# Tile 0's scores as two products of 64 stationary columns, moved in front of tile 0's V product

## The chip, the cores and the metric

The kernel runs on one core of one Trainium2 chip. The metric is the device time of one execution in microseconds (us), the median of several runs.

Five engines work side by side: TensorE (PE: matrix products and transposes; PEld is its loading of stationary operands), VectorE (DVE), ScalarE (ACT), GpSimd (POOL) and SyncE (SP, which issues most of the DMAs). Each takes its instructions in the program's order.

## What is computed

Block-causal attention with 8 batches, 8 heads, 576 positions and a head size of 64, followed by a mixture of 8 experts, of which each position takes one:

```python
scores = scale * np.matmul(q, k.transpose(0, 1, 3, 2))
mask = block_i >= block_j
scores = np.where(mask, scores, -1000000000.0)
attn = np.exp(scores - np.max(scores, axis=-1, keepdims=True))
attn = attn / (np.sum(attn, axis=-1, keepdims=True) + 1e-09)
attn_out = np.matmul(attn, v)
...
expert_idx = np.argmax(x @ w_gate, axis=1)
for e in range(E):
    xe = x[expert_idx == e]
    out[expert_idx == e] = gate_w * (np.maximum(xe @ w1[e], 0.0) @ w2[e])
```

A block has 64 positions, so the 576 positions are 9 blocks. All of it is in float32 or in float32 split into two parts.

## The kernel before, in words

**Attention** works on 32 pairs of heads (m = 0 to 31, 4 pairs for each batch). The 9 blocks of a head are cut into tile 0 (the first 64 positions) and tiles 1 to 4 (128 positions each). The operations of a pair are named steps, and the table `ORDER` (line 414) writes them out by hand. `run` (line 360) goes through the table once per turn, 36 turns in all; an entry such as `S0:3` does step S0 for the pair m = turn - 3. So a turn works on several pairs at once, and pair m has its step with the number 3 in turn m + 3. No scheduler moves anything: the order of the table is the order of each engine's instructions. Entries that begin with z or y let in single steps of the experts' routing and of weight preparation.

The steps that matter here:

- `ld` (line 97, SyncE): loads qd (the queries, with the first block of the keys behind them), kd and v of a pair. qd has three buffers, so the load for pair m waits until the last reader of pair m - 3 is done. That reader is S0 of pair m - 3, in the same turn.
- `pQ` (line 109, GpSimd): scales 640 columns of qd into q. q has two buffers, so this waits for S0, the last reader of the q from two pairs earlier, in the same turn too.
- `S0` (line 157, TensorE): tile 0's scores. The 128 stationary columns of q are head a's 64 positions and head b's 64; in each, the rows of the other head are zero, so one product over all 128 rows gives both heads' scores, one above the other (128 x 64). A float32 product is two TensorE instructions (two passes).
- `S1` to `S4` (line 160): scores of tiles 1 to 4, head a on the rows 0 to 63 and head b on 64 to 127.
- `T..` (line 215): transposes of the exponentials, 128 stationary columns; `H..` (line 244) copies them from PSUM on ScalarE or VectorE. Ta1 is the group directly behind V5 and O0; Tt0 is tile 0's transpose.
- `V0` to `V4` and `V5` (line 253): products with the values. Each is one product for head a and one for head b, each with 64 stationary columns; head a writes the PSUM partitions 0 to 63, head b 64 to 127. V5 is tile 0's: both of its products have 64 moving columns.
- `O0` (line 279, VectorE) copies V5's result out; `M0` (VectorE) takes the maximum of S0's scores, `E0` (ScalarE) their exponential; `Z` (GpSimd) scales tile 0's exponentials into p.

The results of V5, S0, F1 and, in a second allocation, F2 and F0 lie in one PSUM bank (tag o2, one buffer, `part`, line 121). Whichever of S0 and V5 comes first in a turn opens the bank anew and waits for the readers and writers of the turn before.

A turn begins with the last exponential of the pair before (E3B) and ends with the V products V0 to V4. In front of V5 on TensorE thus stand the products of V4, and S1 to S3 ahead of V0.

When a batch is done, `sink` (line 1514) puts its next work in the queues: after the first batch (in turn 7) ten zero fills (line 1517: nine of 256.5 KB and a single row) and three loads of weights (line 1502) on SyncE's queue, behind the load of that turn.

**The experts** (from line 1570 on) come after the attention, with their own loops; the change doesn't touch them.

Of the kernel before, what the change touches and what calls it, by code (L numbers as in the profile page):

```python
# [17 lines left out]
P = 128  # L18
H = 8
S = 576  # L20
D = 64
# [17 lines left out]
class Attention:  # L39
# [113 lines left out]
    def op_S(self, m, i):  # L153

        mm = self.nc.tensor.matmul
        q, k = self.qs[m], self.raws[m][1]
        if i == 0:
            mm(self.part(1, m, "S0", 432, 496), q[:, 512:], self.raws[m][0][:, 512 + P :], start=True, stop=True)  # L158
            return
        e = 64 + 128 * i  # L160
        for c in range(2 if i == 4 else 1):
            for j in range(2):
                out, _ = self.region(m, i, j)
                if i == 4:
                    out = out[:, c]
                n = out.shape[-1]
                o = (0 if j else S - e) + n * c
                r = slice(64 * j, 64 * j + 64)
                ins = mm(  # L169
                    out, q[r, 128 * (i - 1) : 128 * i], k[r, o : o + n], start=True, stop=True, skip_group_check=True  # L170
                )
                self.uses(m, i, j, ins)
# [239 lines left out]


ORDER = """
E3B:3 V5:4 z2:0 O0@D:4 ld:0 Ta1:3 O@A:4 Ha1@A:3 S0:3 S4:2 z6:0 M0:3 Tb1:3 Tk0:3 pQ:1 K4B:2 E0:3 R1:3 K4A:2 z1:0 M4B:2
R2:3 F1:4 Hb1@A:3 Ta2:3 Hk0@A:3 X1:4 Y1:4 M4A:2 Tb2:3 F2:4 E4B:2 y0:0 Z:3 Hb2@D:3 F0:4 Ha2@A:3 Y2:4 z4:0 Tx3:3 Tt0:3
E4A:2 X2:4 S1:2 z5:0 z0:0 z3:0 Ht0@A:3 Y0@D:4 S2:2 K1A:2 K2A:2 S3:2 K1B:2 Hx3@A:3 K2B:2 V0:3 V2:3 M2A:2 K3A:2 M1B:2
M3A:2 E2A:2 E1B:2 V1:3 y1:0 E3A:2 V3:3 M1A:2 K3B:2 M2B:2 E1A:2 M3B:2 V4:3 E2B:2
# [1174 lines left out]
```

## Time and profile before

| | us |
|---|---|
| median of 3 runs | 817.57 |
| the three runs | 817.12, 817.57, 820.97 |
| the profiled execution | 815.47 |
| its span in the profile | 813.7 |
| TensorE busy | 785.0 (96%) |
| VectorE busy | 474.0 (58%) |
| ScalarE busy | 399.5 (49%) |
| GpSimd busy | 391.5 (48%) |

The profile is of one execution; its times count from the start of its span, and 1.8 us of the execution lie outside of it. Busy shares are means over the attention half (to about 372 us) and the expert half. TensorE's records overlap, since products are pipelined: the distance from one start to the next is what a product costs in a row of products, and its duration is longer than that. A number in square brackets behind a row is idle time of the engine before it, and what ended it.

### The profile page before, as it was taken

The numbers are of one execution on the slowest core, as the hardware profiler recorded it, in microseconds if no ns is written. First come the engines' busy times: TensorE is split into PE (matmuls) and PEld (weight loads), VectorE is DVE, ScalarE is ACT, GpSimd is POOL, SyncE is SP. The second block draws the span as 40 slices with busy tenths as digits, with TensorE's granted clock in tenths as the row PEclk, the third lists the DMA queues.
The fourth block names the chain that finished last, engine by engine and source line by source line (L and its number), as shares of the span: only waits on it lengthen the run. The fifth ranks groups of instructions, "written<-read, shape, count | busy, mean of one in ns | idle before, by whom it ended". The sixth has DMA issues, their size and how long they took to land.

```text
span 813.7 us, 17547 instructions
## 1 busy us (share of the span) xinstructions
PE 785.0 (96%) x4524; PEld 590.0 (73%) x4524; DVE 474.0 (58%) x1316; ACT 399.5 (49%) x1016; POOL 391.5 (48%) x397
## 2 busy tenths in 40 slices
PE   4999999999999999998999999999999999999995
PEld 2667666667776666666878888888888888888873
DVE  3666666776767677756846764412244713566953
ACT  3777777777787777762432333232332222332231
POOL 4122243344444361435456766555555556656753
PEclk9999999999999999999999999999999999999999
DMA  4239843536363626541447676744455654667772
GB/s 164 97 101 168 203 125 125 120 121 166 118 156 104 153 76 153 161 120 31 151 120 213 204 209 172 230 131 122 119 154 181 171 182 119 194 210 234 224 214 63
DMA packets 71120, 123.65 MB, mean 152 GB/s; under 512 B 16449, under 2 KB 37697, under 8 KB 70978
## 3 DMA queue, kind: packets, MB, share of 16 engines
q1 hardware_dynamic: 49858, 87.84, 38.2%
q0 software_dynamic: 7680, 20.50, 8.1%
q10 hardware_dynamic: 13440, 13.78, 6.3%
q8 instruction: 45, 0.74, 0.4%
q14 instruction: 97, 0.79, 0.3%
HBM read 73.09 MB, written 21.98 MB: 117 GB/s over the span
## 4 chain that ended last, share of the span: by engine, by line
PE 69%; issue 10%; POOL 9%; DMA 5%; ACT 2%; ACTq 1%; SPq 1%; DVE 1%; POOLq 1%; DVEq 0%
PE py L1170 14%; PE o L270 11%; PE pt L1009 7%; PE ya L169 7%; PE o L1009 4%; PE ph L1009 4%; PE xa L169 4%; PE o L305 4%; POOL low L1143 3%; POOL out L1192 2%; DMA xd<-xg 2%; ACTq L1120 1%; DMA qd<-qT 1%; ACT pb L200 1%; PE o L299 1%
## 5 line engine op out<-in xcount | busy, mean ns | idle before, releaser
L1170 PE MATMUL py<-w,low 128*128 (+1 forms) x912 | 219.7, 396 | 3.2 <-POOL low L1143 1.9
L1170 PEld LDWEIGHTS py<-w,low 128*128 128x128 f32 x912 | 170.5, 187 | 45.6 <-POOL low L1143 2.3
L112 POOL TENSOR_SCALAR q<-qd 128x640 f32<-128x640 f32 x32 | 57.9, 1810 | 188.4 <-PE o L158 124.3
L1188 ACT ACTIVATE y<-py,gates 128x512 f32<-128x512 f32 x35 | 24.1, 689 | 190.7 <-issue 106.3
L1143 POOL TENSOR_TENSOR low<-high,low 128x512 fp32r<-128x512 f32 x69 | 98.0, 1442 | 12.5 <-ACT low L1135 12.1
L1009 PE MATMUL pt<-w,high 128*128 x408 | 98.0, 395 | 0.0
L1009 PEld LDWEIGHTS pt<-w,high 128*128 128x128 f32 x408 | 76.4, 187 | 18.6
L1331 DVE TENSOR_TENSOR w<-raw,w 128x1024 f32 x48 | 74.1, 1582 | 0.0
L200 ACT ACTIVATE pb<-ya,neg 128x320 f32<-128x320 f32 (+2 forms) x96 | 50.0, 524 | 48.1 <-DVE neg L185 48.1
L1087 DVE STREAM_TRANSPOSE hblk<-xg 128x512 f32<-128x512 f32 x35 | 24.8, 710 | 82.5 <-DMA xg<-xd,idx 79.1
L169 PE MATMUL ya<-kd,q 64*128 64x192 f32 (+2 forms) x192 | 61.8, 457 | 2.7 <-ACT pb L200 2.7
L169 PE MATMUL yb<-kd,q 64*128 64x192 f32 (+2 forms) x192 | 61.8, 456 | 0.0
L1328 DVE CAST w<-raw 128x1024 f32 x48 | 52.8, 1140 | 15.1 <-issue 13.2
L695 POOL DMA_INDIRECT tab<-toks,posi x40 | 41.5, 1036 | 28.5 <-DVE run L662 14.8
L1099 DVE STREAM_TRANSPOSE hblk<-pt 128x512 f32<-128x512 f32 x34 | 23.7, 709 | 49.9 <-ACT pt L1046 49.7
L916 POOL DMA_INDIRECT xg<-xd,idx x39 | 43.2, 1108 | 19.3 <-POOL idx L908 18.0
L978 POOL TENSOR_TENSOR xl<-high,xh 128x512 fp32r<-128x512 f32 x16 | 21.2, 1328 | 62.0 <-ACT xh L968 62.0
L200 ACT ACTIVATE pb<-yb,neg 128x192 f32<-128x192 f32 (+2 forms) x96 | 49.7, 525 | 0.2 <-DVE neg L185 0.2
L978 POOL TENSOR_TENSOR high<-high 128x512 fp32r<-128x512 f32 x17 | 24.3, 1431 | 50.5 <-ACT high L968 50.5
L169 PE MATMUL xa<-kd,q 64*128 64x288 f32 x128 | 41.6, 447 | 6.5 <-POOL q L112 6.5
L1135 ACT CAST low<-high 128x1024 fp32r<-128x1024 f32 x35 | 36.5, 1043 | 19.0 <-DMA high<-hblk 17.6
L1192 POOL DMA_INDIRECT out<-y,idx x35 | 38.8, 1108 | 12.9 <-ACT y L1188 5.5
(1015 smaller groups left out, 1760.9 us busy)
## 6 DMA issues: line engine op xcount, KB each, us to landing
raw<-w SPq DMA_DIRECT2D x52, 512.0 KB, 4.7
high<-hblk SPq DMA_DIRECT2D x280, 48.0 KB
high<-hblk ACTq DMA_DIRECT2D x280, 48.0 KB
qd<-qT SPq DMA_DIRECT2D x32, 352.0 KB, 3.6
v<-vt SPq DMA_DIRECT2D x32, 352.0 KB, 4.6
kd<-kT SPq DMA_DIRECT2D x32, 288.0 KB, 3.7
xd<-xt SPq DMA_DIRECT2D x7, 1026.0 KB, 8.4
xd<-xg SPq DMA_DIRECT2D x9, 256.5 KB, 12.8
```

Of the source, the lines that this page charges most:

```text
L112: self.nc.gpsimd.tensor_scalar(q, self.raws[m][0][:, 0 : 512 + P], 0.125, None, ALU.mult)
L169: ins = mm(out, q[r, 128 * (i - 1) : 128 * i], k[r, o : o + n], start=True, stop=True, skip_group_check=True)
L200: ins = self.nc.scalar.activation(dst, src, AF.Exp, bias=self.neg[m][:, c : c + 1], scale=1.0, accum_out=self.sums[m][:, c : c + 1])
L270: self.nc.tensor.matmul(out[r], self.raws[m][2][:, slot], self.ph[m, bank][:, c0:c1], start=t in (0, 5), stop=t in (4, 5), skip_group_chec ...
L916: pool.indirect_dma_start(out=self.xg[i], out_offset=None, in_=self.xd[:, :], in_offset=bass.IndirectOffsetOnAxis(ap=self.idx[:, t : t + 1 ...
L978: pool.tensor_sub(xl, r, xh).then_inc(sem["xp"], 1)
L1009: m = pe.matmul(ph[f], x[:, P * k : P * k + P], weights(k, f, part), start=start and k == 0, stop=stop and k == 3,)
L1143: engine.tensor_sub(hl[:, c], h[:, c], hh[:, c]).then_inc(sem["ln" if engine is pool else "le"], 1)
L1170: m = pe.matmul(self.py[t % 2], h[:, c // 4, P * (c % 4) : P * (c % 4) + P], wf[:, bass.ds(off + (base + 512 * c), 512)], start=n == 0, st ...
L1192: pool.indirect_dma_start(out=self.out[:, :], out_offset=bass.IndirectOffsetOnAxis(ap=(self.router.first if t < EARLY else self.idx)[:, t ...
L1328: dve.tensor_copy(part(c, 0), raw[c % 4]).then_inc(sem["wh"], 1)
L1331: dve.tensor_sub(part(c, 1), raw[c % 4], part(c, 0)).then_inc(sem["wd"], 1)
```

## The change

S0 is no longer one product of 128 stationary columns. It is two of 64, one for each head: head a's columns of q write the partitions 0 to 63, head b's 64 to 127, and both have the same 64 moving columns. It is still computed over all 128 rows with the same zeros. In the table S0 moves from its place between Ta1 and S4 to the place in front of V5.

```diff
         if i == 0:
-            mm(self.part(1, m, "S0", 432, 496), q[:, 512:], self.raws[m][0][:, 512 + P :], start=True, stop=True)
+            out = self.part(1, m, "S0", 432, 496)
+            for j in range(2):
+                r = slice(64 * j, 64 * j + 64)
+                mm(out[r], q[:, 512 + 64 * j : 576 + 64 * j], self.raws[m][0][:, 512 + P :], start=True, stop=True)
             return
...
 ORDER = """
-E3B:3 V5:4 z2:0 O0@D:4 ld:0 Ta1:3 O@A:4 Ha1@A:3 S0:3 S4:2 z6:0 M0:3 Tb1:3 Tk0:3 pQ:1 K4B:2 E0:3 R1:3 K4A:2 z1:0 M4B:2
+E3B:3 S0:3 V5:4 z2:0 O0@D:4 ld:0 Ta1:3 O@A:4 Ha1@A:3 S4:2 z6:0 M0:3 Tb1:3 Tk0:3 pQ:1 K4B:2 E0:3 R1:3 K4A:2 z1:0 M4B:2
```

The lines behind the first hunk stand 3 further down in the changed kernel (S4 is L172 there, V L273, the transposes L242).

TensorE's order from V4 of pair 16 to S4 of pair 18, with what each instruction waits for (a semaphore is named by the engine that raises it, DMAHW by a DMA queue). Before (V5 is the product out of h, S0 the one out of qd and q, Ta1 the row pt17a):

```order
L270 MATMUL o_2646<-ph16a_2618,v_2096 64x128
L270 MATMUL o_2646<-ph16b_2615,v_2096 64x128
L270 MATMUL o_2674<-h_130,v_2096 64x64 [waits DVE_49,PE_49]
L270 MATMUL o_2674<-h_130,v_2096 64x64
L239 MATMUL pt17a_2687<-ident,pb_2584 128x128 [waits Activation_49]
L239 MATMUL pt17a_2687<-ident,pb_2584 128x128 x3
L158 MATMUL o_2674<-qd_2247,q_2433 128x64 [waits DMAHW2_49,DVE_49]
L169 MATMUL xa_2697<-kd_2397,q_2575 128x288 [waits DMAHW2_49]
L169 MATMUL xb_2699<-kd_2397,q_2575 128x288 [waits Activation_49]
```

And in the changed kernel:

```order
L273 MATMUL o_2663<-ph16a_2635,v_2111 64x128
L273 MATMUL o_2663<-ph16b_2632,v_2111 64x128
L161 MATMUL o_2691<-qd_2263,q_2449 64x64 [waits DMAHW2_49,DVE_49,PE_49]
L161 MATMUL o_2691<-qd_2263,q_2449 64x64
L273 MATMUL o_2691<-h_130,v_2111 64x64 x2
L242 MATMUL pt17a_2706<-ident,pb_2601 128x128 [waits Activation_49]
L242 MATMUL pt17a_2706<-ident,pb_2601 128x128 x3
L172 MATMUL xa_2715<-kd_2414,q_2592 128x288 [waits DMAHW2_49,DVE_49]
L172 MATMUL xb_2717<-kd_2414,q_2592 128x288 [waits Activation_49]
```

S0's two products stand between V4 and V5 and have taken over V5's waits; S4 stands directly behind the transposes and has a wait for VectorE that S0 had covered.

VectorE's order at O0 (L281, L284 in the changed kernel) and M0 (the reduction out of o), in the same turn. Before:

```order
L281 COPY o_134<-o_2674 128x64 [waits PE_49]
L575 TENSOR_REDUCE L_2677<-lg_2156 128x32
L185 TENSOR_REDUCE neg_2582<-o_2674 128x1 [waits PE_49]
L180 MEMSET xb_2699 64x64 [waits PE_49,Activation_49]
L206 TENSOR_TENSOR rs_2583<-sums_2581,eps 128x9 [waits Activation_49]
```

And in the changed kernel:

```order
L284 COPY o_134<-o_2691 128x64 [waits PE_49]
L578 TENSOR_REDUCE L_2696<-lg_2170 128x32
L188 TENSOR_REDUCE neg_2599<-o_2691 128x1
L183 MEMSET xb_2717 64x64 [waits PE_49,Activation_49]
L209 TENSOR_TENSOR rs_2600<-sums_2598,eps 128x9 [waits Activation_49]
```

Nothing changes places there; M0 no longer waits for TensorE, since O0 ahead of it waits for a later product.

## Rows read from the trace of the kernel before

**Rows 1.** Stretches: window, busy time of each engine, granted clock, DMA share, GB/s

```profile
17.20:20.80 3.60, 3.53 (x14) 2.43 (x14) 0.59 (x2) 2.13 (x8) 1.81 (x1) 1.00 0.27 65
26.00:86.00 60.00, 60.00 (x449) 40.59 (x446) 39.43 (x153) 45.83 (x142) 11.36 (x11) 1.00 0.56 121
98.00:340.00 242.00, 241.90 (x1845) 168.19 (x1842) 169.18 (x692) 184.62 (x562) 101.69 (x97) 1.00 0.50 136
```

**Rows 2.** Timeline of TensorE in turn 20: start, duration, instruction, [idle before]

```profile
204.52 0.27 PE L270 MATMUL o<-ph16a,v 128*64 128x128 f32 x1
...
204.63 0.27 PE L270 MATMUL o<-ph16a,v 128*64 128x128 f32 x1
...
204.74 0.28 PE L270 MATMUL o<-h,v 128*64 128x64 f32 x4
204.79 0.23 PE L270 MATMUL o<-h,v 128*64 128x64 f32 x2
204.95 0.66 PE L239 MATMUL pt17a<-ident,pb 128*128 128x128 f32 x4
205.34 0.27 PE L239 MATMUL pt17a<-ident,pb 128*128 128x128 f32 x1
205.45 0.34 PE L158 MATMUL o<-qd,q 128*128 128x64 f32 x2
205.72 0.51 PE L169 MATMUL xa<-kd,q 64*128 64x288 f32 x1
```

**Rows 3.** Timeline of TensorE, later in this turn and at the next V5

```profile
207.38 0.60 PE L239 MATMUL pt17k<-ident,pb 128*128 128x128 f32 x4
207.82 0.66 PE L305 MATMUL o<-fold,oT 128*128 128x144 f32 x4
...
210.44 0.27 PE L236 MATMUL pt17t<-ident,p 128*64 128x128 f32 x1
210.65 0.43 PE L169 MATMUL ya<-kd,q 64*128 64x192 f32 x1
...
215.53 0.28 PE L270 MATMUL o<-h,v 128*64 128x64 f32 x4
```

**Rows 4.** Chain of work that ended last, turns 7 to 9: start, length, what

```profile
62.88 0.19 PE o L158 x2
...
63.12 0.33 SPq L104
...
68.28 13.27 DMA xd<-xg
...
81.62 7.22 DMA qd<-qT
```

**Rows 5.** Timeline of TensorE in turn 9, the transpose of pair 6

```profile
91.28 0.30 PE L236 MATMUL pt6t<-ident,p 128*64 128x128 f32 x1 [1.61 <-POOL p L213]
```

**Rows 6.** Timeline of TensorE, the router's small products in turn 21

```profile
219.15 0.24 PE L611 MATMUL o<-oh,ones 128*128 128x32 bf16 x4
219.25 0.31 PE L239 MATMUL pt18a<-ident,pb 128*128 128x128 f32 x1
```

**Rows 7.** Timelines of VectorE and GpSimd around S0 in turns 20 and 21

```profile
205.07 0.23 DVE L281 COPY o<-o 128x64 f32<-128x64 f32 x1 [0.33 <-PE o L270]
...
207.12 0.11 DVE L180 MEMSET xb<- 64x64 f32 x1 [1.07 <-PE xb L169]
...
216.61 0.23 DVE L185 TENSOR_REDUCE neg<-o 128x1 f32<-128x64 f32 x1 [0.53 <-PE o L158]
...
205.94 1.81 POOL L112 TENSOR_SCALAR q<-qd 128x640 f32<-128x640 f32 x1 [6.00 <-issue]
```

**Rows 8.** Timeline of TensorE in turn 3

```profile
17.27 1.11 PE L239 MATMUL pt0a<-ident,pb 128*128 128x128 f32 x4 [2.13 <-ACT pb L200]
...
18.64 0.85 PE L169 MATMUL xa<-kd,q 64*128 64x288 f32 x1
```

**Rows 9.** Chain of work that ended last, turns 33 and 34

```profile
355.14 2.70 ACT pb L200 x10
357.84 0.31 ACT oT L277
```

## The prediction

> **What bounds the kernel now.** The table of stretches comes first: from 26 to 86 us and from 98 to 340 us, the attention half, TensorE is busy all the time (60.00 of 60.00, 241.90 of 242.00) [rows 1]. There nothing counts but the length of TensorE's own row of products, and it counts in full, turn for turn. A turn is 10.79 us (tile 0's V product starts at 204.74 and in the next turn at 215.53 [rows 2, 3]).
>
> Next, the turn itself, product by product [rows 2]. Tile 4's V products (64 stationary columns) run as pairs of head a and head b: one pair at 204.52, the next at 204.63. Tile 0's V product (V5) is four instructions, two passes for each of two heads, with the same 64 stationary columns: one pair at 204.74, the other at 204.79, and at 204.95 the transposes, which use all 128 columns. Then the scores of tile 0 (S0, two passes, 128 stationary columns) from 205.45 to 205.79, and S4, on 64 rows, at 205.72. Two things are to be seen. Where the tiling changes, the next product starts only 0.07 us before the end of the last one: V5 ends at 204.74 + 0.28 = 205.02, the next starts at 204.95; S0 ends at 205.79, the next starts at 205.72; a transpose elsewhere ends at 210.44 + 0.27 = 210.71, the next starts at 210.65 [rows 3]. Where it doesn't change, the next starts long before the end: V5's pairs are 0.055 us apart, with durations of 0.23.
>
> Last, the chain of work that ended last, between 62 and 91 us [rows 4]. It doesn't run through TensorE there: it goes from the end of S0 of pair 4 (62.88 + 0.19) into SyncE's queue, where the load of the next qd waits for the buffer that S0 is the last to read (63.12), then through the zero fill that is queued behind that load (it lands at 68.28 + 13.27 = 81.55), the next load of qd (81.62, 7.22 us), and GpSimd's scaling q and small step p, to the transpose Tt0 at 91.28, before which TensorE was idle for 1.61 us [rows 5].
>
> **The change, part by part.**
>
> *S0 taken out from between the transposes and S4.* Today S4 starts at 205.72. Without S0 it is the last transpose (205.34 + 0.27 = 205.61) that the new tiling waits for, so S4 starts 0.06 to 0.07 before that, at 205.54 or 205.55 [rows 2, 3]: **0.175 us less** in a turn.
>
> *S0 put between V4 and V5.* It is then four instructions, two passes for each of two heads, with 64 stationary and 64 moving columns on 128 rows: what V5 is, instruction for instruction. V5's pairs are 0.055 us apart, and V5 follows V4 at V4's own pace (0.11 us), with no gap for the tiling. Two more pairs cost 2 x 0.055 = **0.11 us more**. Bounds from the rows: nothing below 0.10 (four small products of the router, from 219.15 to the next thing at 219.25 [rows 6], are the closest in these rows), and 0.22 if the heads don't run beside each other. I take 0.11, since the nearest row is the very neighbour, of equal shape.
>
> Net per turn: 0.175 - 0.11 = **0.065 us less**.
>
> A rule stands against this part. What the trace shows first: the router's four products start 0.025 us apart [rows 6], and the eight of V4's last pairs and V5 take from 204.52 to 204.95, 0.054 us each with a change of tiling in it [rows 2]. The Trainium skill, "TensorE: Matmul & The Clock Gate", section "Wait — 56ns, not 53.3ns?", says that with hardware decode off the sequencer spends some 62 ns on each matmul, which binds once the array's work is shorter. By that the four small products would cost 0.25 us instead of 0.11, and a turn would get 0.07 longer instead of shorter; both rows disagree with it.
>
> *The waits.* S0 now opens the bank of the small products, so it carries the two waits that V5 had (for VectorE's copy and TensorE's last product of the turn before in that bank), and V5 has none. In front of V5 they show no idle time: 204.74 follows 204.63 at the pace of the pairs. S0 is rid of its wait for VectorE's copy O0 (205.07 + 0.23 = 205.30 [rows 7]), which it met before 205.45 anyway. S4 gets a wait for a fill of the turn before, long past. Nothing for all of these.
>
> *V5 0.11 us later against V4.* Behind it hang O0 and then M0 on VectorE. M0 now waits for S0 (0.53 us idle in the row at 216.61) and will no longer, and after M0 VectorE is idle for 1.07 us until the next scores [rows 7]. That cover takes the 0.11; were it gone, the 0.11 would come back into VectorE's row, which TensorE doesn't wait for in these stretches. Nothing.
>
> *GpSimd and SyncE.* GpSimd's scaling q and SyncE's load of qd both wait for S0 of the same turn. S0's end moves from 205.79 to where V5's second pair ends now, 204.79 + 0.23 = 205.02: **0.77 us earlier**. GpSimd had been idle for 6.00 us before q [rows 7], and q is used a turn later: nothing. But in turn 7 the load stands at the head of the chain above [rows 4], and each step behind it, up to Tt0 at 91.28, waits for the one before. I take the whole 0.77; the bounds are nothing, if the transfers are held by something that doesn't move, and 0.77. TensorE still waits there: it arrives only about 0.7 us earlier itself, and of the 1.61 about 1.0 is left. What it saves in turns 7 to 9 goes into that wait and isn't counted.
>
> *The first turn with S0 (turn 3).* There is no V5 yet. TensorE is idle for 2.13 us before the transposes at 17.27, and S0 falls into that. Products take longer there (S4's first 0.85 us, against 0.51 later [rows 2, 8]). S4 moves from 18.64 to 17.27 + 1.11 - 0.07 = 18.31: **0.33 us less**, and what follows hangs on the products behind S4. If ScalarE's copies take half of it up, 0.16.
>
> *The end.* In turn 34 the chain is ScalarE's queue (ten exponentials from 355.14 to 357.84, and its copies behind them [rows 9]), so that turn's saving isn't counted; all turns before it lie ahead of those exponentials.
>
> **Sum.** 0.33 (turn 3) + 3 x 0.065 (turns 4 to 6) + 0.77 (turn 7's load) + 24 x 0.065 (turns 10 to 33: 1.56) = **2.86 us less**. The profiled execution took 815.47 us, 2.1 below the median of the runs, 817.57. Against its own time the sum gives 812.6; against the median, which is what will be compared, **814.7 us**, 0.35% less. About 0.5% (4.1 us) is what a measurement of this kernel can tell from no change; the forecast is inside that.
>
> **Rivals.**
>
> *The start gets fast sooner.* The products between 17.27 and 20.8 us take nearly twice as long as later ones, though the granted clock reads 1.00 there as elsewhere, the level of 2.4 GHz [rows 1, 8]; so the profile doesn't tell why. They come after an idle stretch, and S0 now fills a part of it. If that made these 3.6 us fast, up to 1.8 more would go: 812.9, 0.57% less. Nothing shows that it would. Chance 0.07.
>
> *The four products go one by one.* At 0.055 each they cost 0.22, and a turn gets 0.045 longer. With 27 turns 1.2 more, less 0.33 and the 0.66 that remain of turn 7's lead: 817.8. The pairs of V5 speak against it. By the page above it would come out a little slower still. Chance 0.05.
>
> *The gain gets lost.* The transfers of turn 7 don't move, and the waits of the expert half take up what is left: 817.6. For it: three runs of the kernel before lie 3.9 us apart. Chance 0.11.
>
> *S0 drains the array on both sides.* If S0 counted as a tiling of its own next to V4 and V5, each change would cost what the change behind V5 does: 0.10 before it (0.16 from V5's second pair to the transposes, instead of 0.055) and 0.06 behind it (0.50 us for the four transposes there, 0.44 for four in the middle [rows 2, 3]). Two of these are 0.32 a turn, net 0.255 more: 27 x 0.255 = 6.9, less 0.33 and some 0.5 left of turn 7's lead: 6.0 longer, 823.6, slower by 0.7%. Any drain of over 0.065 us a turn makes the turn longer. Against it: V4 to V5, with these shapes, shows none. Chance 0.05; with waits that I don't see, slower has 0.07.
>
> **How the numbers follow.** The forecast has 0.70. Its savings run from 1.9 us (turn 7's load moves nothing, turn 3 half: 27 x 0.065 + 0.16) to 3.1 (0.10 for the new place), which is 814.5 to 815.7, and medians of this kernel scatter by some 2 us around that. To hold 8 in 10 the range reaches down past the first rival and up past the second and third: 811.5 to 818.5; the fourth is left out. Faster by over 0.5%: the first rival and a fifth of the forecast, by scatter, 0.22. Slower by over 0.5%: 0.07. Within: 0.71.
>
> **What would show it.** Right: S0's two pairs 0.055 us apart between V4 and V5; S4 directly behind the transposes, 0.06 to 0.07 before the last one's end; turns of 10.72 us instead of 10.79; q 0.77 us earlier in its turn; Tt0 of pair 6 some 1.3 us earlier, with 1.0 us of idle time before it; the end of attention 2.9 us earlier. Wrong: a gap of 0.1 at either edge of S0; that Tt0 earlier by no more than TensorE's own savings; or an expert half that is longer by what attention saved.

## The result, and the profile after

The changed kernel takes 823.17 us (median of 19 runs, 820.58 to 827.25), the kernel before 817.57 (19 runs, 815.06 to 821.39). The comparison of the runs puts the ratio at 1.0055 [1.0043, 1.0067]: about **4.5 us slower**, outside the range of the prediction, and with the sign that had 7 in 100. The profiled execution took 823.59 us, 8.1 more than that of before.

TensorE does what was predicted, almost to the number. Its timeline in turn 20 of the changed kernel (compare [rows 2]; L161 is S0, L273 the V products, L242 Ta1, L172 S4):

```profile
206.58 0.27 PE L273 MATMUL o<-ph16a,v 128*64 128x128 f32 x1
...
206.69 0.28 PE L161 MATMUL o<-qd,q 128*64 128x64 f32 x4
206.81 0.29 PE L273 MATMUL o<-h,v 128*64 128x64 f32 x4
207.03 0.66 PE L242 MATMUL pt17a<-ident,pb 128*128 128x128 f32 x4
207.61 0.51 PE L172 MATMUL xa<-kd,q 64*128 64x288 f32 x1
...
217.54 0.29 PE L273 MATMUL o<-h,v 128*64 128x64 f32 x4
```

S0's four instructions take 0.12 us between V4 and V5 with no gap for the tiling. From the first product behind V4 to S4 it is 206.69 to 207.61, 0.92 us, against 204.74 to 205.72, 0.98, before. The turn is 10.73 us instead of 10.79. But not every turn: here is V5 of four turns from turn 12 on, and a product that waits for VectorE in two of them (F2, L308).

```profile
118.59 0.29 PE L273 MATMUL o<-h,v 128*64 128x64 f32 x4
...
129.34 0.29 PE L273 MATMUL o<-h,v 128*64 128x64 f32 x4
...
134.16 0.73 PE L308 MATMUL o<-fold,oT 128*128 128x144 f32 x4 [0.21 <-DVE lg L327]
...
140.62 0.29 PE L273 MATMUL o<-h,v 128*64 128x64 f32 x4
...
145.41 0.73 PE L308 MATMUL o<-fold,oT 128*128 128x144 f32 x4 [0.34 <-DVE lg L327]
...
151.95 0.29 PE L273 MATMUL o<-h,v 128*64 128x64 f32 x4
```

The two turns behind 129.34 take 11.28 and 11.33 us; in the kernel before, the same two take 11.01 and 10.79 (V5 at 128.77, 139.78 and 150.57). F2 starts 0.33 and 0.50 us later, against the products ahead of it, than in the first experiment below, and that is 0.83 of the 0.93 us that the two turns lose against it; the idle time in brackets is less, since a product's record reaches beyond the start of the next. The list of groups by line and shape (group, count, busy us, mean ns) says where VectorE lost the time. Before:

```profile
L206 DVE TENSOR_TENSOR rs<-sums,eps 128x9 f32<-128x9 f32 x32 | 4.8, 150 | 0.6 <-ACT p L200 0.6
```

And after:

```profile
L209 DVE TENSOR_TENSOR rs<-sums,eps 128x9 f32<-128x9 f32 x32 | 12.7, 396 | 1.1 <-ACT p L203 1.1
```

This is R1, the sum of 9 columns with a constant, `rs = sums + eps`. The change doesn't touch it, and in all it takes 8 us more. The timelines of GpSimd and VectorE in turn 13 show how. Before:

```profile
129.91 1.81 POOL L112 TENSOR_SCALAR q<-qd 128x640 f32<-128x640 f32 x1 [6.02 <-PE o L158]
131.70 1.26 POOL L1512 TENSOR_TENSOR high<-xg,zero 128x512 fp32r<-128x512 f32 x1
...
131.15 0.11 DVE L180 MEMSET xb<- 64x64 f32 x1 [1.07 <-PE xb L169]
131.17 0.15 DVE L206 TENSOR_TENSOR rs<-sums,eps 128x9 f32<-128x9 f32 x1
```

And after:

```profile
129.62 1.81 POOL L112 TENSOR_SCALAR q<-qd 128x640 f32<-128x640 f32 x1 [5.45 <-PE o L161]
131.41 1.26 POOL L1515 TENSOR_TENSOR high<-xg,zero 128x512 fp32r<-128x512 f32 x1
...
131.54 0.11 DVE L183 MEMSET xb<- 64x64 f32 x1 [1.52 <-PE xb L172]
131.57 1.12 DVE L209 TENSOR_TENSOR rs<-sums,eps 128x9 f32<-128x9 f32 x1
```

Behind q stands, in turns 13, 14, 17, 18, 21, 22, 25 and 26, a weight step (y0, in turn an addition and a subtraction of two operands in SBUF, 1.26 us). Before, R1 fell into q and took 0.15 us; the weight step began 0.53 us later. Now q starts earlier against V5 (0.28 us behind it instead of 1.14), so the weight step begins at 131.41, 0.16 ahead of R1, and R1 lasts until 132.69, the end of the weight step (131.41 + 1.26 = 132.67). What VectorE does next is a microsecond late, and F2's products wait for it. The Trainium skill, "SBUF — State Buffer", section "SBUF: two separate sides", states this: a VectorE instruction with two SBUF inputs and a GpSimd instruction that reads SBUF exclude each other, whichever starts first holds the shared ports for its whole length, and "the other fully blocks". The trace agrees for R1 against the weight step. It doesn't against q, which reads SBUF too: R1, begun 1.2 to 1.6 us into q's 1.81, took 0.15 us there in 28 turns of the kernel before.

The second place is in the expert half. Chain of waits of the changed kernel (start, length, what): the eight transfer issues that ScalarE makes ahead of a late tile of tokens,

```profile
419.48 0.62 ACTq L1123
...
420.13 0.86 ACTq L1123
...
421.03 0.61 ACTq L1123
...
422.31 1.59 ACTq L1123
```

and the timeline of TensorE behind them,

```profile
427.12 1.19 PE L1012 MATMUL ph<-w,xh 128*128 x4 [1.45 <-ACT xh L957]
```

where the kernel before has

```profile
422.65 1.19 PE L1009 MATMUL ph<-w,xh 128*128 x4 [0.20 <-issue]
```

and the stretches around it (columns as in [rows 1]; the third row is the stretch of the kernel before that belongs beside the second):

```profile
420.00:427.00 7.00, 5.68 (x25) 4.23 (x23) 4.01 (x6) 0.80 (x2) 0.00 (x0) 1.00 0.55 146
427.00:432.00 5.00, 4.50 (x13) 3.28 (x14) 1.75 (x3) 2.80 (x5) 3.91 (x5) 0.71 0.53 156
...
423.20:428.20 5.00, 4.62 (x20) 3.49 (x19) 2.42 (x3) 2.12 (x4) 4.27 (x5) 1.00 0.61 190
```

One issue takes 1.59 us instead of some 0.61, TensorE waits 1.45 us for the copy queued behind it (0.20 before), and after the wait the granted clock falls to 0.71 for a stretch, which is a part of it at the level of 1.2 GHz. In the kernel before, the eight issues take 5.40 us together, here 6.62. The view of the DMA queues from 419 to 426.5 us has a row that the same stretch before has not:

```profile
q8 instruction: 1, 0.02, 1.2%
```

It is a load of program code (16 KB). (A second such row there, of q14, stands in the same stretch of kernels without the long issue too.) The change adds two products a pair, each a weight load and a matmul: 128 more instructions for TensorE, all ahead of this place. Measured from the same late product, these loads come at -1, +24 and +42 us before, and at about -7 to -15, +10 and +33 after; the eight issues stand at +9 to +14. From that product on (the 1700th from the end) the next 120 take 30.83 us instead of 27.98. That is the largest such difference of all profiles: in the six other kernels below with a load in these issues the granted clock stays at 1.00 behind the wait, and the 120 products take 28.5 to 29.1 us.

The third place is turn 9, where Tt0 of pair 6 waits at the end of the chain of transfers [rows 4, 5]:

```profile
90.26 0.30 PE L239 MATMUL pt6t<-ident,p 128*64 128x128 f32 x1 [2.36 <-POOL p L216]
```

It comes 1.0 us earlier than before, with 2.36 us of idle time instead of 1.61. The load of turn 7 was issued 2.35 us earlier (60.77, not 63.12), but the next qd landed only 1.0 earlier (87.83, not 88.84): the transfers took 27.1 us instead of 25.7. And behind the wait the granted clock is low:

```profile
90.20:94.00 3.80, 3.74 (x15) 1.70 (x17) 1.27 (x8) 1.48 (x5) 0.01 (x1) 0.63 0.29 102
94.00:97.00 3.00, 3.00 (x20) 1.28 (x18) 1.80 (x6) 2.61 (x10) 0.00 (x0) 0.90 0.06 21
```

Turn 9 takes 15.14 us, 12.81 before. In one profiled execution each that is: first V5 1.3 us earlier (28.34, not 29.64), attention from first to last V5 4.4 longer (340.01, not 335.58: +3.8 for the late F2, +2.3 for turn 9, -1.7 for the shorter turns), 2.9 in the expert half at the late tile, and some 2 in its last products, the last 60, which take between 18.1 and 22.6 us in all kernels run here and which I can't attribute. What of this belongs to the change, and what to this one execution, the profiles alone don't tell.

### The profile page after: what moved, and what is told of

It is laid out like the page before. It is cut to its first block, busy times and chain, and to the rows that moved or that the text cites. A ratio compares the mean times of both kernels' runs of the same rounds, so it can differ in the third digit from the quotient of the medians.

```text
span 821.8 us, 17674 instructions
## 1 busy us (share of the span) xinstructions
PE 787.0 (96%) x4588; PEld 585.8 (71%) x4588; DVE 476.1 (58%) x1316; ACT 402.7 (49%) x1016; POOL 386.9 (47%) x397
## 4 chain that ended last, share of the span: by engine, by line
PE 77%; DMA 5%; DVE 4%; issue 4%; SPq 3%; ACTq 2%; ACT 2%; POOL 2%; DVEq 1%; POOLq 0%
PE py L1173 20%; PE o L273 11%; PE pt L1012 10%; PE ya L172 7%; PE ph L1012 6%; PE o L1012 6%; PE xa L172 4%; PE o L308 3%; ACTq L1123 2%; DMA xd<-xg 2%; SPq L1123 1%; DVE rs L209 1%; DMA qd<-qT 1%; ACT pb L203 1%; DMA out<-y,idx 1%
## 5 line engine op out<-in xcount | busy, mean ns | idle before, releaser
L1146 POOL TENSOR_TENSOR low<-high,low 128x512 fp32r<-128x512 f32 x69 | 93.1, 1373 | 12.8 <-ACT low L1138 12.2
L1331 DVE CAST w<-raw 128x1024 f32 x48 | 58.0, 1248 | 15.9 <-issue 15.9
L1334 DVE TENSOR_TENSOR w<-raw,w 128x1024 f32 x48 | 65.7, 1408 | 0.0
L172 PE MATMUL ya<-kd,q 64*128 64x192 f32 (+2 forms) x192 | 62.8, 462 | 2.7 <-ACT pb L203 2.7
L172 PE MATMUL yb<-kd,q 64*128 64x192 f32 (+2 forms) x192 | 62.8, 462 | 0.0
L308 PE MATMUL o<-fold,oT 128*128 128x144 f32 x256 | 44.0, 294 | 3.4 <-DVE lg L327 2.7
L172 PE MATMUL xa<-kd,q 64*128 64x288 f32 x128 | 40.6, 438 | 6.6 <-POOL q L112 6.6
L188 DVE TENSOR_REDUCE neg<-yb 128x1 f32<-128x192 f32 (+2 forms) x96 | 42.8, 474 | 3.3
```

Of the source, the lines that this page charges most:

```text
L172: ins = mm(out, q[r, 128 * (i - 1) : 128 * i], k[r, o : o + n], start=True, stop=True, skip_group_check=True)
L308: mm(t[:, i], self.oT[m, 0][:, o : o + P], w, start=True, stop=True)
L1146: engine.tensor_sub(hl[:, c], h[:, c], hh[:, c]).then_inc(sem["ln" if engine is pool else "le"], 1)
L1331: dve.tensor_copy(part(c, 0), raw[c % 4]).then_inc(sem["wh"], 1)
L1334: dve.tensor_sub(part(c, 1), raw[c % 4], part(c, 0)).then_inc(sem["wd"], 1)
```

## The experiments

Twelve kernels ran in three groups, each beside runs of the kernel before on the same chip (their medians: 820.77, 823.5 and 821.68 us; chips differ, so ratios are compared, not times), 4 to 12 runs each. The changed kernel itself was not run again on these chips: where a run is set against its 1.0055, it is assumed that this ratio carries over. Free of that are the kernels made from the kernel before, and pairs of one group. The theories: **R1 held** (3.8 us by the profile), **the code load** in ScalarE's issues, and **turn 9**, the transfers of turn 7 with the low clock behind them. The rival to all: that S0's new place itself costs TensorE time.

### The weight step behind Z (changed kernel)

```diff
-... F2:4 E4B:2 y0:0 Z:3 Hb2@D:3 ...
+... F2:4 E4B:2 Z:3 y0:0 Hb2@D:3 ...
```

> The changed kernel with one swap in the table: GpSimd's weight or scatter step y0 stands behind Z instead of ahead of it. Theory A (in eight turns a weight subtraction or addition on GpSimd now starts within 0.2 us ahead of VectorE's small sum R1 and holds it for 1.1 us instead of 0.15, and F2's products on TensorE wait for VectorE behind it, 0.2 to 0.4 us a turn and the same again in the turn after): R1 takes 0.15 us in all 32 turns, the idle times before F2 are gone, the pairs of turns of 11.28 and 11.33 us become about 10.96 and 10.73, and the kernel gets some 3 us shorter than the changed one, 820 against 823.2. Rival (R1's length is a symptom; F2 waits for something else, such as the bank): the idle times stay and the time is 823.

Measured: 821.94 us, ratio 1.0008 [0.9991, 1.0025]; 0.0047 less than the changed kernel's 1.0055, 3.9 us (0.0047 x 817.57). R1 by line and shape is back:

```profile
L209 DVE TENSOR_TENSOR rs<-sums,eps 128x9 f32<-128x9 f32 x32 | 4.8, 150 | 1.1 <-ACT p L203 1.1
```

F2 no longer waits, and the two turns are 10.96 and 10.72 us (V5 at 133.61, 144.57 and 155.29) instead of 11.28 and 11.33: 0.93 for the pair, and with the other three pairs (0.92 to 0.97) 3.76 us, the size that was measured. But its profiled execution took 824.02 us, because of turn 9, here 17.58 us long:

```profile
94.55 0.36 PE L239 MATMUL pt6t<-ident,p 128*64 128x128 f32 x1 [4.80 <-POOL p L216]
```

So turn 9 varies with S0 in the same place; its wait in one profile says nothing of the change.

### q behind Z in turn 9 alone (changed kernel)

Z's scaling p, for which Tt0 waits, stands on GpSimd behind q, and q behind the load. In turn 9 the order is turned round:

```diff
+        def at_turn(turn, order):
+            if turn != 9:
+                return order
+            rest = [x for x in order if x[0] != "pQ"]
+            n = rest.index(("Z", 3)) + 1
+            return rest[:n] + [("pQ", 1)] + rest[n:]
...
-            for name, lag in order:
+            for name, lag in at_turn(turn, order):
```

> The changed kernel; in turn 9 alone GpSimd's scaling q stands behind Z, so that the transpose Tt0 of pair 6 no longer waits for the load of qd that is late there. Theory A (the wait of 2.36 us there is what drops TensorE's clock to half for some 3 to 4 us): no idle time before that transpose, granted clock 1.00 from 88 to 97 us, turn 9 at 10.7 us instead of 15.1, some 4 us less than the changed kernel, 819, if the next q isn't late for S4 in turn 10. R1 is still held in eight turns. Rival (the late load is only met one step later, at S4 of turn 10): the same wait is there, and 823.

Measured: 819.64 us, 0.9986 [0.997, 1.0002], 0.0069 less than the changed kernel, 5.7 us. Turn 9 takes 10.96 us; TensorE is busy throughout at a granted clock of 1.00 (stretch view):

```profile
88.00:97.00 9.00, 9.00 (x71) 5.66 (x70) 6.04 (x29) 6.56 (x21) 3.62 (x2) 1.00 0.73 243
```

The kernel before has 7.38 us of products there. R1 stays held in the eight turns. Turn 9's wait is thus worth more than the whole difference of the two kernels; whether it is worth more in the changed one, the last group bears on.

### q behind Z in every turn (changed kernel, and before)

```diff
-... Tk0:3 pQ:1 K4B:2 ... y0:0 Z:3 Hb2@D:3 ...
+... Tk0:3 K4B:2 ... y0:0 Z:3 pQ:1 Hb2@D:3 ...
```

> The changed kernel with GpSimd's scaling q behind Z in every turn, and y0 therefore ahead of both. Theory A (the held R1 and the wait of turn 9 are what the change costs): both are gone, R1 0.15 us in every turn, turns of 10.73 (10.96 with the router's products), 7 us less than the changed kernel: 816, or 0.2% below the kernel before. Rival (the loss lies in the expert half or in the start): less than 3 us of it come back, 820 or more.

> The kernel before with the same reordering of q behind Z in every turn. Theory A: turn 9's wait of 1.6 us goes, nothing else moves on TensorE, since R1 isn't held in the kernel before either: about 816, 1.6 less. If the reordering by itself is worth as much here as it is on the changed kernel (the rival: it removes a cost that has nothing to do with the change), 811 to 812.

Measured: 823.08 us, 1.0035 [1.002, 1.0049], and 822.01 us, 1.0026 [1.0009, 1.0043]. Both missed what was expected. R1 took 0.15 us and turn 9 was cured, but now the weight steps are early, and other small instructions of VectorE meet them. Timelines of GpSimd, VectorE and TensorE in the changed kernel so edited:

```profile
133.47 1.26 POOL L1515 TENSOR_TENSOR high<-xg,zero 128x512 fp32r<-128x512 f32 x1
...
133.89 0.87 DVE L679 TENSOR_SCALAR g<-g 128x5 f32<-128x5 f32 x1
...
138.32 0.55 PE L242 MATMUL pt11a<-ident,pb 128*128 128x128 f32 x3 [0.43 <-ACT pb L203]
```

Five columns take 0.87 us, to the end of the weight step, and TensorE has six waits of 0.43 to 0.70 us (0.54 to 0.82 in the kernel before). Two more are longer there: `oh<-cd,w` (128x40) takes 0.90 us on average over eight instead of 0.20, `at<-w,base` (128x5) 0.56 instead of 0.18. Turning GpSimd's order round for all turns moves the meeting to other instructions; which of the three holds TensorE up was not tried.

### R1 late, with nothing changed on TensorE (before)

```diff
-... Tk0:3 pQ:1 K4B:2 E0:3 R1:3 K4A:2 z1:0 M4B:2
-R2:3 F1:4 ...
+... Tk0:3 pQ:1 K4B:2 E0:3 K4A:2 z1:0 M4B:2
+R1:3 R2:3 F1:4 ...
```

> The kernel before with VectorE's small sum R1 moved two operations later (behind M4B, directly ahead of R2), so that it starts inside GpSimd's weight additions and subtractions without any change on TensorE. Theory A (the two engines can't run these two kinds of operation at once, and what F2 waits for is VectorE behind it): R1 takes 0.8 to 1.1 us instead of 0.15 in the same eight turns (13, 14, 17, 18, 21, 22, 25, 26), TensorE idles before F2 there, and the attention half gets 2 to 4 us longer. Rival (R1 got long because of the earlier GpSimd scaling q or because of S0's shape): R1 stays at 0.15 and nothing changes.

Measured: 828.33 us, 1.0044 [1.002, 1.0067], 3.6 us: a loss like that of R1 in the changed kernel, with S0 where it was. By line and shape:

```profile
L206 DVE TENSOR_TENSOR rs<-sums,eps 128x9 f32<-128x9 f32 x32 | 11.9, 373 | 0.5 <-ACT p L200 0.5
```

R1 is held in the same eight turns (up to 1.09 us), F2 waits 0.30 to 0.43, and the pairs of turns are 0.97 to 1.03 longer than in the kernel before, 4.0 us in all. Its turn 9 waits 4.39 us in the profile, again with the old S0. At the end of attention its profile has another 2.4 us (F2's waits there are 0.93 and 1.27 us instead of 0.57 and 0.48); whether R1's place does that too was not tried.

### The move alone, and the split alone

First the product of 128 columns in front of V5, then two products of 64 at the old place behind the transposes:

```diff
-            out = self.part(1, m, "S0", 432, 496)
-            for j in range(2):
-                ...
+            mm(self.part(1, m, "S0", 432, 496), q[:, 512:], self.raws[m][0][:, 512 + P :], start=True, stop=True)
```

```diff
-E3B:3 S0:3 V5:4 z2:0 ... Ha1@A:3 S4:2 ...
+E3B:3 V5:4 z2:0 ... Ha1@A:3 S0:3 S4:2 ...
```

> The move alone: S0 as one product of 128 stationary columns, in front of V5. Theory A: on TensorE two more changes of tiling, some 0.3 us a turn more than the changed kernel (turns of 10.95 to 11.05); GpSimd's q is early as in the changed kernel, so R1 is held in the same turns; the program has as many TensorE instructions as before, so the code load of TensorE's queue stays outside of ScalarE's transfer issues, and the wait near 427 us is 0.2 us as in the kernel before. In all 6 to 9 us slower than before, 824 to 827 for 817.6. Rival for the expert half (its wait comes from when the attention ends): 1.0 to 1.5 us of wait there.

> The split alone: S0 as two products of 64 stationary columns, at its old place between the transposes and S4. Theory A: one more change of tiling, so turns of about 10.9 us instead of 10.79; q isn't early, R1 is 0.15 us in all turns; but there are 128 more TensorE instructions, so the code load falls into ScalarE's issues as in the changed kernel: one issue of 1.3 to 1.6 us instead of 0.6, TensorE idle for about 1 us near 427 us, granted clock below 1 behind it. In all 3.5 us from the turns and 2 from the expert half: 823. Rival (the wait comes from when the attention ends): 0.2 us of wait there, and 821.

Measured: the move alone 833.78 us, 1.0125 [1.0099, 1.0151], with turns of 11.13 us; the split alone 830.04 us, 1.0088 [1.0059, 1.0116], with turns of 10.88. TensorE with the move alone,

```profile
213.79 0.27 PE L270 MATMUL o<-ph16a,v 128*64 128x128 f32 x1
...
214.00 0.43 PE L158 MATMUL o<-qd,q 128*128 128x64 f32 x2
214.37 0.34 PE L270 MATMUL o<-h,v 128*64 128x64 f32 x4
214.63 0.66 PE L239 MATMUL pt17a<-ident,pb 128*128 128x128 f32 x4
```

and with the split alone:

```profile
211.45 0.66 PE L242 MATMUL pt17a<-ident,pb 128*128 128x128 f32 x4
212.03 0.34 PE L161 MATMUL o<-qd,q 128*64 128x64 f32 x4
212.30 0.51 PE L172 MATMUL xa<-kd,q 64*128 64x288 f32 x1
```

With 128 columns S0 stands 0.21 us behind V4, and V5 0.37 behind S0; with 64 the two steps are 0.11 and 0.12. So the product of 128 columns costs more at this place: its turn is 0.34 us longer than in the kernel before and 0.40 longer than in the changed one, and the change avoids that by making both parts at once. Turns and time are above what was expected (10.95 to 11.05 us, 6 to 9 us more; 0.0125 is 10.2). At the late tile it has no load in the issues and a wait of 0.16 us, as expected. The split alone adds 0.09 a turn, 2.5 us over 28 turns; its 7.2 us hold besides the code load (an issue of 1.09 us, a TensorE wait of 0.67) and a turn 9 that waited 4.27 us in its profile. 2 to 3 us are left; in its profile the copy O0 at the end of attention starts 2.2 us after V5's last product ended (0.05 in the kernel before), and F2 waits 2.56 us for it instead of 0.57. What held the copy the profile doesn't show.

### The code loads put back (changed kernel), and moved (before)

Ahead of all else, 32 products of 8 by 8 columns of a tile of zeros are added, 128 instructions; nothing uses their result.

```diff
+        pad = att.ps_t.tile([P, 512], F32, tag="pt", name="pad")
+        for _ in range(32):
+            nc.tensor.matmul(pad[0:8, 0:8], att.zero[:, 0:8], att.zero[:, 0:8], start=True, stop=True)
```

> The changed kernel with 32 products of 8 by 8 columns on a zero tile ahead of everything on TensorE, where it is idle for 6.5 us: 128 more TensorE instructions, another half of a 16 KB code load. They compute nothing that is used. Theory A: the code loads stand, against the expert half, where they do in the kernel before, so ScalarE's issues are 0.6 us each and TensorE waits 0.2 to 0.4 us near 427 us without a fall of the clock, 2 us less in the expert half than the changed kernel; R1 is held as there. If these products also quicken the first turns, V5 of pair 0 starts earlier than at 28.3, by up to 4 us. Rival (the wait near 427 us has nothing to do with the code load): one issue of over 1.2 us stays.

> The kernel before with the 32 small products ahead of everything: its TensorE program is as long as the changed kernel's. Theory A: the code load moves by half a block into ScalarE's issues, one of them takes 1.3 us or so instead of 0.6, TensorE waits 0.7 to 1.4 us near the first late tile of the experts and runs slower behind it, some 2 us more, a ratio of 1.0015 to 1.003, without any change in the attention. Rival: no wait there, ratio 1.

Measured: the changed kernel 822.91 us, 0.9996 [0.9974, 1.0018], though R1 is held in it as before the edit; the kernel before 824.08 us, 1.0039 [1.0023, 1.0055]. The loads move as the theory has it, and the first turns don't get faster (first V5 at 30.20 and 29.52 us). The changed kernel with the products has no q8 row at its eight issues, they take 5.41 us, and TensorE's wait behind them is gone:

```profile
426.00 1.19 PE L1012 MATMUL ph<-w,xh 128*128 x4 [0.18 <-issue]
```

The kernel before with the products has the q8 row there, one issue of 1.21 us, and the wait:

```profile
426.41 1.18 PE L1009 MATMUL ph<-w,xh 128*128 x4 [0.86 <-ACT xh L954]
```

So 32 products that nobody needs make one kernel faster by 0.0059 and the other slower by 0.0039, the second more than was expected. With the next group (0.0029) that is 2.4 to 4.8 us (0.0059 x 817.57) for where the code loads fall. At the late tile the profiles show less: six of the seven kernels with a load there lose 0.5 to 1.2 us in the 120 products, the changed kernel 2.9. From there to the last 60 products all kernels agree within 0.1 us. The rest of the effect is thus not located; the same shift also moves the loads against the transfers of turn 7, and the two larger figures are of kernels in which turn 9 still waits.

### The cures together

The weight step behind Z and q behind Z in turn 9, in the changed kernel; the same with the 32 products; and turn 9's order alone in the kernel before. The edits are those above.

> As the kernel with all three cures, but without the 32 small products. Theory A: the code load falls into ScalarE's issues again, one of them takes 1.3 to 1.6 us, TensorE waits for about 1 us there and its granted clock is below 1 behind it: 2 us more than with all three. Rival (the code load costs nothing net): the same time as with all three.

> The changed kernel with all three cures: GpSimd's q behind Z in turn 9, y0 behind Z in every turn, and 32 small products ahead of everything. Theory A: R1 0.15 us everywhere, turns of 10.73 and 10.96, no wait before Tt0 in turn 9, about 0.2 us of wait near the first late tile of the experts: what is left of the change is its 0.06 us a turn (1.7 in all) and the cure of turn 9. Against the kernel before: 1.7 and what turn 9 costs there (2 to 5 us) less, a ratio of 0.992 to 0.9955. Rival (there is a further loss in the change that I have not found): 0.997 or more.

> The kernel before with the cure of turn 9 alone. Theory A (the wait there is of the kernel before too, of a length that varies from run to run, and of a fall of the clock when it is over 2 us): 2 to 5 us less than before, a ratio of 0.994 to 0.9975; the kernel with all three cures is still 1.7 us below this one. Rival (the wait is the change's doing): 1.6 us less at the most, 0.998.

Measured: 816.61 us, 0.995 [0.9932, 0.9968]; with the products 814.41 us, 0.9921 [0.9904, 0.9939]; the kernel before with turn 9's order 814.78 us, 0.9919 [0.9901, 0.9937]. The stretch of turn 9 in the last:

```profile
88.00:97.00 9.00, 9.00 (x67) 5.67 (x66) 6.21 (x28) 6.89 (x23) 2.87 (x2) 1.00 0.92 305
```

Three things follow. Turn 9 costs the kernel before 0.0081, 6.6 us and more than was expected, as much as the changed one (5.7): no part of the difference by these two, which come from two chips. The two profiles of the comparison itself have 1.8 (12.81 - 11.02) and 4.2 us (15.14 - 10.96) there, so that some of the 4.5 us lies in turn 9 isn't excluded. The code load costs 2.4 us between the first two, which differ in the 32 products alone: the eight issues take 6.02 us and TensorE waits 0.87, against 5.39 with no q8 row. The granted clock behind that wait stays at 1.00, other than expected. Of the 2.4 us between their two profiles 0.8 lies at the late tile and 1.8 in the last 60 products, in which there is scatter of that size. And with all three cured the changed kernel should be 1.7 us ahead of the kernel before with its turn 9 cured. In the profiles it is: 331.99 us from first to last V5 against 333.79. In the medians it isn't to be seen, 0.9921 against 0.9919, with intervals of 0.0036. Whether the shorter turn is worth its 1.7 us in the end stays open.

## Why the prediction was wrong

By the steps of the prediction:

- **S0 taken out, and put in front of V5: right.** Net 0.06 us a turn, forecast 0.065; 28 turns give -1.7 us. S0 in front of V5 takes 0.12, forecast 0.11. The Trainium skill's 62 ns for each matmul with hardware decode off ("TensorE: Matmul & The Clock Gate", section "Wait — 56ns, not 53.3ns?"), weighed there, would give an estimate of 0.25 for the four; the rows have 0.12. No run shows which decode was in use.
- **The waits, and V5 later: right by themselves.** M0 and O0 met nothing.
- **"GpSimd and SyncE" is the step that failed.** It said that q 0.77 us earlier, used a turn later, costs "nothing". q is indeed early and its result isn't missed. But moving an instruction moves those queued behind it on its engine. Counted from V5's start in turn 13, the weight step came from 2.93 us to 2.07, and R1 only from 2.40 to 2.23; so the two changed order. That R1 is held while the weight step runs, that this costs 0.9 to 1.0 us in each of four pairs of turns, and that nothing else is needed for it, was shown from both sides: cured in the changed kernel (-3.9 us), made in the kernel before (3.6 us against runs on the same chip, 4.0 by its turns).
- **"V5 0.11 us later": the cover was there, and beside the point.** VectorE's idle 1.07 us ahead of R1 [rows 7] was taken as cover against lateness; it is 1.52 us in the changed kernel. The question was what else runs when R1 starts; I had the row of q, and not the one behind it.
- **Turn 7's load, -0.77: not to be seen.** It started earlier, by 2.35 us (0.87 of it against V5, the rest with the whole turn), and gave 1.0 in the one profile, with 2.36 us of idle time where 1.0 was forecast. In turn 9 the wait lay between 1.61 and 4.80 us over the profiles, with old and new S0, and behind most of these waits TensorE's granted clock falls (last section). A term of 0.77 at the end of such a chain has no place in a sum.
- **Turn 3, -0.33: right at S4, lost behind it.** Where the products there are slow as in the kernel before, S4 starts at 18.32 or 18.33 us with S0 in its new place and at 18.63 or 18.64 with it in the old one. But first V5 lies at 29.52 to 30.32 us with the kernel before's program and at 28.34 to 30.20 with the changed one's. In the profile of the changed kernel the products were fast from 17.3 us on, as the first rival had it. That isn't S0's doing: in six other profiles they are fast at 17.3 us too, two of them with S0 in the old place (one of these without the 32 products). In those six the granted clock falls soon behind (0.81 on average from 17 to 26 us), in the changed kernel's it doesn't, and no other profile has so early a V5.
- **Not in the prediction at all:** 128 more instructions move TensorE's code loads against ScalarE's issues; +2.4 us by the pair that differs in this alone, of which the late tile shows 0.8.

The sum by measured terms: +3.8 (R1) + 2.4 (code load) - 1.7 (turns) = +4.5 us, and the runs give 4.5. That it agrees so closely is luck: the code load was also measured at 3.2 and 4.8, the 1.7 us are seen in profiles and not in medians, and what turn 9 adds in this comparison isn't known. What is shown is that the held R1 costs 3.6 to 4.0 us, whatever the rest.

Of the rivals, the one with S0 draining the array on both sides gave 823.6, next to the time that came. It was wrong nonetheless: S0 shows no gap at either edge. A cost of the size that it names (0.255 us a turn net) shows only where S0 keeps its 128 columns: 0.34 in the move alone.

## What to carry to other kernels

An instruction that starts earlier pulls forward what is queued behind it on its engine: before writing "nothing", look at the next two instructions there and at what the engines beside it start in that time, above all short VectorE sums against GpSimd's long ones. A row of products that shrinks by 0.5% is worth less than one collision that it causes, and the collision can be mended alone (here by exchanging two entries). And where a change alters the number of instructions, compare the code loads in the DMA view at the places that hang on a queue of issues: 32 unused products moved three pairs of kernels by 0.3 to 0.6%.

## What the runs showed of the hardware that was not expected

- R1 under a weight step takes 0.82 to 1.18 us instead of 0.15 (all 40 cases in five profiles), to the weight step's end, and never under q (115 cases, each begun 1.1 us or more into q), though both are GpSimd instructions that read SBUF; a VectorE addition of a constant to 5 columns took 0.87.
- One ScalarE issue of a transfer takes 1.1 to 1.6 us instead of some 0.61 where a code load of 16 KB passes. Of the 14 kernels with a profile, the seven that have a load in these issues have TensorE waits of 0.67 to 1.45 us behind them, and the seven that have none 0.22 at most. What in the load lengthens the issue was not tried.
- A wait can cost more than itself, and its length alone doesn't tell whether it does. In turn 9 waits of 2.36 us and, in five other profiles, of 2.70 to 4.80 us were followed by products at a granted clock of 0.50 to 0.69 over the next 3.8 to 4.6 us, so a good part at the 1.2 GHz level; one of 1.61 us (the kernel before) and one of 2.45 (the changed kernel with the 32 products; 1.00 from 92.1 to 95.9 us) were not, and at the late tile one of 1.45 us was. With the fall, 2.36 us of waiting made turn 9 4.2 us longer; without it, 2.45 made it 2.6 longer. So the 2 us that the last expectation above names as a threshold isn't borne out.
